# Fewer idle products around chunk 0, and modulation rows picked from 32 rows

## The chip, the cores and the metric

The kernel runs on one core of one Trainium2 chip. The metric is device time in microseconds (us): the time of one execution on the core. For the kernel before, three timed runs gave 661.33, 662.86 and 663.32 us; the median is 662.86 us.

A core has five engines that run side by side and wait for one another through semaphores: PE (TensorE, matrix products), DVE (VectorE), ACT (ScalarE), POOL (GpSimd) and SP (SyncE, which here issues nearly all DMAs). PE reads from the on-chip memory SBUF and writes to PSUM, where DVE and ACT fetch its results.

## The reference

One sequence of S = 2048 positions and D = 640 channels. A condition vector c gives six modulation rows of 640 values each; two blocks follow, each with its own layer norm, scale, shift and gate.

```python
mod = (_silu(c) @ w_mod).reshape(c.shape[0], 6, 1, -1)
sa, ca, ga, sb, cb, gb = (mod[:, 0], mod[:, 1], mod[:, 2], mod[:, 3], mod[:, 4], mod[:, 5])
h = _layernorm(x, axis=-1) * (1 + ca) + sa
x = x + ga * _A_ref(h, A_k, A_v, A_shift_k, A_ssm_k, A_ssm_D)
h = _layernorm(x, axis=-1) * (1 + cb) + sb
x = x + gb * _B_ref(h, B_w1, B_b1, B_w2, B_b2)
```

`_A_ref(q, k, v, ...)` runs a short convolution of four taps over k, multiplies by v, convolves each channel over the whole sequence with its own kernel of 2048 values (by an FFT), adds kv times a per-channel D, and multiplies by q. `_B_ref` is an MLP over the sequence axis: 2048 to 1728, GELU, and back.

## The kernel before, in words

All data are float32. An f32 product on PE leaves two pairs of records in the trace (weight load and MATMUL, twice); products in the form fp32r, used in the MLP, leave one pair.

**Block A** works in five chunks of 128 channels. The long convolution is a transform in two steps, written as products with constant matrices:

- k*v of a chunk is made by `kv_ops` (DVE, partly POOL; every elementwise product and sum of two tensors goes through the helper on L57). Its scratch on DVE is the PSUM tile `tap`: columns 0 to 512 hold a running sum, columns 512 to 768 the four taps, which `taps()` writes (ACT, L174).
- Step one, `step1(side, t)` (PE L223, ACT copies the result out on L229): four groups t for the k*v side (0) and four for the kernel side (1). The kernel side reads tile `p`, which `perm` (ACT, L168) fills.
- Step two, `f2(g)` for g = 0 to 7 (PE L242): 32 products each. ACT copies half of the result to `kt` (L246), DVE multiplies (`mul`, two products into `p`), and POOL or DVE adds into `y`.
- Back: `i2(r)` for r = 0, 1 (PE L271; ACT copies out on L280, DVE in one case on L278), then `i1(half)` for two halves (PE L291). `gate` (DVE, then POOL) multiplies by the normalized and modulated q, which `a1_ops` prepares (ACT L298, DVE), and adds to x.

The pieces of neighbouring chunks are interleaved by hand in the loop over c: during chunk c, DVE makes the k*v of a later chunk, taken piece by piece from the list `fill` by `dv(n)`; at the end of a turn step one of the next chunk's kernel runs. PSUM has four buffers of 1024 columns: `tap`, and three that `psum()` hands out in turn, so a product waits until the readers of the buffer's last contents are done.

**Modulation.** `mod_load` (SP, L344) loads w_mod in five parts; `mod_part` (PE L356) sums the products with silu(c) in `tap`, with each of three modulation rows held alike in 32 partitions, at partitions 0, 32 and 64; `mod_sum` (ACT L360) copies them to SBUF. `mod_row(i)` (PE L367) spreads row i over all 128 partitions by a product with a selection column from `pick`: two products, one for each half of 320 columns. Rows 0 to 2 are made at the end of chunk 0; rows 3 to 5 after chunk 4.

**Idle products.** `idle(n, ps)` (PE L350) issues n f32 products of 128 columns whose results nobody reads. In the turn of chunk 0 they stand ahead of `i2(0)`, and ahead of and behind the second `i1`, all writing to `tap`; in chunk 4 ahead of `mod_part`. A loop on L863 issues 34 fp32r products of 320 columns ahead of block B's first products.

**Block B** then runs the MLP as products of matrices split into high and low parts (PE L450, L990, L1307, L1384), from about 282 us to the end.

What sets the order: the program's own order on each engine, since the schedule is written by hand; SP issues its DMAs in that order too, each when its target is free.

Of the kernel before, what the change touches and what calls it, by code (L numbers as in the profile page):

```python
# [47 lines left out]
def mixer_kernel(ctx: ExitStack, tc: tile.TileContext, q, k, v, shift_k, ssm_k, ssm_D, w1, b1, w2, b2, c,  # L48
# [7 lines left out]
    act, dve, pool, pe, sync = nc.scalar, nc.vector, nc.gpsimd, nc.tensor, nc.sync  # L56
    TT = lambda eng, o, a, b, op: eng.tensor_tensor(o, a, b, op=op)  # L57
    uid = [0]
# [8 lines left out]
    def psum(slot=None):  # L67

        uid[0] += 1
        slot = ring[uid[0] % len(ring)] if slot is None else slot  # L70
        return psp.tile([128, 1024], F32, name=f"pst_{uid[0]}", tag=f"pst{slot}", bufs=1)
# [28 lines left out]
    F1, V2, ID, OWN = SM[:, 0:256], SM[:, 256:384], SM[:, 384:420], SM[:, 420:422]  # L100
# [6 lines left out]
    def small(n):  # L107
        so[0] += n
        assert so[0] <= 736
        return sm[:, so[0] - n:so[0]]  # L110
# [3 lines left out]
    bst = small(16 * 5 * 6).rearrange("p (j s k) -> p j s k", j=16, s=5)  # L114
    mv = small(32).rearrange("p (j k) -> p j k", j=16)
    rs1, nm1, rs2, nm2, tm = small(16), small(16), small(16), small(16), small(16)
    pick = small(64)
    su, sq, msb = small(16), small(16), small(1)
    epsc = small(1)
    B1C, B2C = cols[:, 0:14], cols[:, 14:30]  # L120
# [1 line left out]
    tap = psp.tile([128, 1024], F32, name="tap", tag="pst3", bufs=1)  # L122
# [92 lines left out]
    def step1(side, t, later=False, x=X, last=False):  # L215

        ps = psum()
        for a in range(8):
            i = 8 * t + a
            lhs = KSP[:, i] if side else x.rearrange("p (i m) -> p i m", i=32)[:, i]  # L220
            o = 256 * (a // 2) + a % 2
            for ri in range(2):
                pe.matmul(ps[64 * ri:64 * ri + 64, o:o + 255:2], lhs, F1[:, 128 * ri:128 * ri + 128], start=True,  # L223
                          stop=True)
        cut = (0, 32, 128) if t == 3 and last else (0, 128)

        def evac():
            for k0, k1 in zip(cut, cut[1:]):
                act.activation(Z[:, side, t, :, k0:k1], ps.rearrange("p (a k e) -> p a k e", a=4, e=2)[:, :, k0:k1], AF.Copy)  # L229
        return evac if later else evac()  # L230

    def f2(g):

        ps = psum()
        for kk in range(8):
            k1 = 8 * g + kk
            for ri in range(2):
                for h in range(2):
                    o = 128 * kk + 64 * ri
                    rhs = bass.AP(tensor=T_z.tensor, offset=T_z.offset + 64 * k1 + 32 * h,  # L240
                                  ap=[T_z.ap[0], [4096, 2], [1, 32]])
                    pe.matmul(ps[64 * h:64 * h + 64, o:o + 64], W2[k1 // 32][:, 2 * (k1 % 32) + ri], rhs, start=True, stop=True)  # L242
        pv = ps.rearrange("p (m s i) -> p m s i", s=2, i=32)
        xs_ = pv[:, :, 0]
        kt = KT[g % 2]
        act.activation(kt.rearrange("p (m i) -> p m i", i=32), pv[:, :, 1], AF.Copy)  # L246
        pa, pb = P[:, 1024 * (g % 2):1024 * (g % 2) + 512], P[:, 1024 * (g % 2) + 512:1024 * (g % 2) + 1024]
        m16 = lambda t: t.rearrange("p (m i) -> p m i", i=32)

        def mul():  # L250
            TT(dve, m16(pa), xs_, m16(kt), ALU.mult)
            sw = bass.AP(tensor=kt.tensor, offset=kt.offset + 32, ap=[kt.ap[0], [64, 8], [-32, 2], [1, 32]])
            TT(dve, pb.rearrange("p (k r i) -> p k r i", k=8, r=2), xs_.rearrange("p (k r) i -> p k r i", r=2), sw,
               ALU.mult)

        def add(eng=pool):
            for ri, t, op in ((0, pa, ALU.subtract), (1, pb, ALU.add)):
                t = t.rearrange("p (k r i) -> p r k i", k=8, r=2)
                TT(eng, Y[:, ri, :, 8 * g:8 * g + 8].rearrange("p i k -> p k i"), t[:, 0], t[:, 1], op)
        return mul, add  # L260
# [86 lines left out]
    def idle(n, ps):  # L347

        for _ in range(n):
            pe.matmul(ps[:, 0:128], F1[:, 0:128], F1[:, 128:256], start=True, stop=True)  # L350

    def mod_part(ps, kk, place):

# [9 lines left out]
    def mod_row(i, t, slot=None, later=False):  # L363

        ps, j = psum(slot).rearrange("p (h m) -> p h m", h=2), i % 3
        for h in range(2):
            pe.matmul(ps[:, h, 0:320], pick[0:96, j:j + 1].to_broadcast([96, 128]),  # L367
                      t[0:96, 320 * h:320 * h + 320], start=True, stop=True)
        ps = ps[:, :, 0:320]
        two = lambda t: t.rearrange("p (h m) -> p h m", h=2)  # L370
        if later:
            return lambda: act.activation(two(GB), ps, AF.Copy)
        if i == 0:
            act.activation(two(G0), ps, AF.Copy)
        elif i == 1:
            act.activation(two(G1), ps, AF.Copy, bias=1.0)
        elif i == 2:
            TT(dve, two(G0), ps, two(G0), ALU.mult)
            TT(dve, two(G1), ps, two(G1), ALU.mult)
        elif i == 3:  # L380
            act.activation(two(SB), ps, AF.Copy, accum_out=msb)
        elif i == 4:
            dve.tensor_scalar(two(CB), ps, 1.0, None, op0=ALU.add)
# [70 lines left out]
    piece = lambda t, n: [t[:, 640 * i:640 * i + 640] for i in range(n)]  # L454
    stg = T_g[0:36, 0:128]
    dve.memset(stg, 0.0)
    dve.memset(pick[0:96, 0:3], 0.0)
    for j in range(3):
        dve.memset(pick[32 * j:32 * j + 1, j:j + 1], 1.0)
    dve.memset(epsc, EPS)  # L460
    for h in range(2):
        dve.memset(KX[64 * h:64 * h + 1, 0:3, :], 0.0)
# [39 lines left out]
    ps = psum()  # L502
# [63 lines left out]
    for c in range(NC):  # L566
# [1 line left out]
        ac, po = a1_ops(c)  # L568
        pend_m = pend_a = None
        for g in range(8):  # L570
            m_, a_ = f2(g)
            if pend_m:
                pend_m()
            if pend_a:
                pend_a()
            pend_a, pend_m = (pend_m and pa_next), m_
            pa_next = a_
            if c:
                for f_ in ac[2 * g:2 * g + 2]:
                    f_()  # L580
            elif 0 < g < 5:
                w2_part(1, (g - 1) % 2, 32 * ((g - 1) // 2), 32)
                if g == 4:
                    load_q(range(4))
                    sync.dma_start(T_v1[:, 0:2048], c_v1, max_dma_last_dim=2048)
                    load_q(range(4, 8))
                    for kk in range(2):
                        mod_load(0, kk, homes[kk])
            if cn is None:

                t, o = (X, T_aux)[g // 4], 512 * (g % 4)
                act.activation(t[:, o:o + 1], epsc, AF.Copy)
                for b in range(2):
                    sync.dma_start(t[64 * b:64 * b + 64, o:o + 512],
                                   dram(w1, (16 * b + g) * F, [[32 * F, 64], [1, 512]]))
            if c == 1 and 1 < g < 6:
                late[g + 2]()
            dv(-(-len(fill) // max((6 if c else 8) - g, 1)))
            if c and cn is not None and g == 3:
                perm_add(cn)  # L600
            if cn == NC - 1 and g in turns:
                mod_third(turns[g])
# [13 lines left out]
        if c == 0:  # L616
# [3 lines left out]
            ps = psum()  # L620
# [1 line left out]
            act.activation(cols, ps[:, 0:36], AF.Copy)  # L622
            act.activation(sil, cols[:, 30:35], AF.Silu)
            step1(0, 1)
            idle(5, tap)
            i2(0)
            step1(0, 2)
            i2(1)
            k0 = step1(0, 3, True)
            for kk in range(4):  # L630
# [48 lines left out]
        if c:  # L679
            dv(7 if cn is not None else 8)  # L680
            if cn == NC - 1:
                mod_third(2)
            i2(0)
            if cn is None:
                split_rows(1, T_aux[:, 0:2048], (0, 1, 3))
                idle(4, psum((uid[0] + 1) % 3))
                uid[0] += 2
                mod_part(tap, 3, pl[3])
                i2(1, dve)
                t = mem("y", 4096, "wb2")  # L690
                blk[2] = j16(t[:, 0:2048]), j16(t[:, 2048:4096])
                break
            run(po)
            if cn == NC - 1:
                mod_third(3)
            step1(0, 2)
            if cn == NC - 1:
                mod_third(4)
            i2(1)
            step1(0, 3)  # L700
            dv(3)
# [3 lines left out]
        if cn == NC - 1:  # L705
            mod_third(5)
        for half in range(2):
            if c == 0 and half:
                idle(5, tap)
            ps = i1(half)  # L710
            if c == 0 and half:
                idle(4, tap)
            if c and half:
                dv(3)
            elif c:
                k0 = step1(1, 0, True)
            elif half:
                run(po[2:4])
            gate(c, ps, half)
# [35 lines left out]
    start = []  # L755
# [103 lines left out]
    ring[:] = [3, s1, s2, s0]  # L859
    uid[0] += 3 - uid[0] % 4  # L860
    acc.append(psum().rearrange("p (h m) -> p h m", h=2))
    for i in range(34):
        pe.matmul(acc[0][:, i % 2, 0:320], blk[0][0][:, 0].bitcast(F32R),  # L863
                  blk[1][0].rearrange("p j m -> p (j m)")[:, 0:320].bitcast(F32R), start=True, stop=True)
    x1_stats(range(2, 4))
# [587 lines left out]
```

## Time and profile before

| what | before |
|---|---|
| timed runs, median (lowest to highest) | 662.86 us (661.33 to 663.32) |
| the profiled execution's own time | 665.26 us |
| its span, first to last instruction | 663.3 us |
| mean granted clock of TensorE | 0.994 |
| busy share PE / DVE / ACT / POOL | 95% / 81% / 50% / 19% |
| idle products L350 (f32, 128 columns) | 36 records |
| `mod_row` products L367 | 24 records |
| products of L863 | 34 records |

How to read it: a row of a timeline gives start and length in us, engine, line, operation, what is written and read, the shape and type, and a count; in brackets stands the engine's idle time before it and who ended it ("issue" if the profile shows nobody). "PE" rows are the products and "PEld" the weight loads, which overlap them. A window row gives each engine's busy time with its instruction count (PE, PEld, DVE, ACT, POOL), then the granted clock of TensorE, the DMA share and GB/s. The chain of waits is followed back from the last instruction, at each step to what released it.

### The profile page before, as it was taken

The numbers are of one execution on the slowest core, as the hardware profiler recorded it, in microseconds if no ns is written. First come the engines' busy times: TensorE is split into PE (matmuls) and PEld (weight loads), VectorE is DVE, ScalarE is ACT, GpSimd is POOL, SyncE is SP. The second block draws the span as 40 slices with busy tenths as digits, with TensorE's granted clock in tenths as the row PEclk, the third lists the DMA queues.
The fourth block names the chain that finished last, engine by engine and source line by source line (L and its number), as shares of the span: only waits on it lengthen the run. The fifth ranks groups of instructions, "written<-read, shape, count | busy, mean of one in ns | idle before, by whom it ended". The sixth has DMA issues, their size and how long they took to land.

```text
span 663.3 us, 21125 instructions
## 1 busy us (share of the span) xinstructions
PE 627.7 (95%) x9131; PEld 590.6 (89%) x9131; DVE 536.3 (81%) x933; ACT 329.7 (50%) x547; POOL 127.0 (19%) x143
## 2 busy tenths in 40 slices
PE   6989779899999999898999999999999999999997
PEld 2878469899999998698997999999999999999997
DVE  7789668979979569799986976576799779888895
ACT  1664365646647655566777553345453133333331
POOL 5762027524226044000000000000000530000000
PEclk9999889999999999999999999999999999999999
DMA  9988997447432336171317342346832726346601
GB/s 188 223 226 244 330 183 159 97 79 165 88 80 82 102 95 185 41 159 32 64 33 223 116 118 80 81 105 173 266 106 57 203 88 194 109 130 172 190 31 40
DMA packets 173516, 88.46 MB, mean 133 GB/s; under 512 B 92430, under 2 KB 163632, under 8 KB 173424
## 3 DMA queue, kind: packets, MB, share of 16 engines
q1 hardware_dynamic: 166252, 85.53, 50.1%
q10 hardware_dynamic: 6916, 1.31, 1.2%
q8 instruction: 71, 1.16, 0.7%
q0 software_dynamic: 256, 0.28, 0.2%
q14 instruction: 21, 0.17, 0.1%
HBM read 73.01 MB, written 14.09 MB: 131 GB/s over the span
## 4 chain that ended last, share of the span: by engine, by line
PE 60%; DVE 21%; DMA 8%; ACT 4%; issue 3%; SPq 3%; ACTq 0%; DVEq 0%
PE pst L1307 16%; PE pst L990 10%; PE pst L1384 7%; PE pst L450 6%; PE pst L223 6%; PE pst L271 5%; PE pst L242 4%; PE pst L291 3%; DVE p L57 3%; SPq L535 2%; DVE tap L57 2%; DMA p<-in_w_mod_dram 2%; DMA xb<-in_A_q_dram 2%; ACT z L280 2%; DVE kt L57 2%
## 5 line engine op out<-in xcount | busy, mean ns | idle before, releaser
L242 PE MATMUL pst<-z,w 128*64 128x64 f32 x2560 | 78.9, 223 | 9.5 <-DVE p L57 4.4
L242 PEld LDWEIGHTS pst<-z,w 128*64 128x64 f32 x2560 | 76.7, 138 | 12.2 <-issue 8.3
L229 ACT ACTIVATE z<-pst 128x1024 f32<-128x1024 f32 (+2 forms) x45 | 43.3, 975 | 41.7 <-PE pst L223 41.6
L57 POOL TENSOR_TENSOR y<-p 128x256 f32<-128x256 f32 x72 | 51.3, 742 | 41.8 <-DVE p L57 41.5
L57 DVE TENSOR_TENSOR p<-pst,kt 128x512 f32<-128x512 f32 x80 | 50.7, 681 | 9.5 <-ACT kt L246 9.4
L1307 PE MATMUL pst<-r_z,m_w 128*128 128x320 f32 x222 | 41.6, 309 | 0.1
L271 PEld LDWEIGHTS pst<-v,y 32*128 32x128 f32 x1280 | 38.2, 187 | 3.8 <-issue 2.9
L271 PE MATMUL pst<-v,y 32*128 32x64 f32 x1280 | 40.3, 272 | 0.7 <-issue 0.5
L974 ACT ACTIVATE s_w<-s_w 128x768 fp32r<-128x768 f32 (+1 forms) x26 | 21.8, 838 | 36.8 <-DVE s_w L57 12.1
L246 ACT ACTIVATE kt<-pst 128x512 f32<-128x512 f32 x40 | 23.9, 597 | 31.0 <-PE pst L242 16.0
L1295 ACT ACTIVATE m_w<-m_v 128x896 fp32r<-128x896 f32 x24 | 22.7, 951 | 32.3 <-PE pst L1307 16.8
L57 DVE TENSOR_TENSOR s_w<-s_w,s_w 128x768 fp32r<-128x768 f32 (+1 forms) x26 | 24.6, 945 | 16.8 <-ACT s_w L974 12.1
L223 PE MATMUL pst<-v,p 128*64 128x128 f32 x640 | 37.4, 274 | 0.3 <-issue 0.2
L223 PEld LDWEIGHTS pst<-v,p 128*64 128x64 f32 x640 | 35.1, 137 | 2.0 <-issue 1.4
L57 DVE TENSOR_TENSOR tap<-tap,kt 128x512 f32<-128x512 f32 x51 | 35.5, 696 | 1.3
L1307 PEld LDWEIGHTS pst<-r_z,m_w 128*128 128x128 f32 x222 | 34.8, 188 | 0.4 <-DVE m_w L57 0.4
L280 ACT ACTIVATE z<-pst 128x512 f32<-128x512 f32 x38 | 21.1, 649 | 25.0 <-PE pst L271 25.0
L223 PE MATMUL pst<-v,x 128*64 128x128 f32 x512 | 30.8, 275 | 1.3 <-DVE x L57 0.9
L57 DVE TENSOR_TENSOR m_w<-m_v,m_w 128x896 fp32r<-128x896 f32 x24 | 27.9, 1167 | 3.3 <-ACT m_w L1295 2.9
L57 DVE TENSOR_TENSOR kt<-in,tap 128x512 f32<-128x512 f32 x42 | 28.8, 685 | 1.2
L223 PEld LDWEIGHTS pst<-v,x 128*64 128x64 f32 x512 | 27.8, 137 | 2.1 <-POOL y L57 1.0
L450 PE MATMUL pst<-r_z,wb 128*128 128x320 f32 x180 | 28.1, 311 | 1.5 <-DVE aux L57 1.3
(373 smaller groups left out, 1564.9 us busy)
## 6 DMA issues: line engine op xcount, KB each, us to landing
m_x<-xs SPq DMA_DIRECT2D x28, 160.0 KB
out_dram<-m_x SPq DMA_DIRECT2D x28, 160.0 KB
aux<-in_A_ssm_k_dram SPq DMA_DIRECT2D x8, 512.0 KB
m_v<-in_B_w_dram SPq DMA_DIRECT2D x9, 448.0 KB
x<-in_B_w_dram SPq DMA_DIRECT2D x7, 448.0 KB
s_w<-in_B_w_dram SPq DMA_DIRECT2D x16, 192.0 KB
in<-in_A_v_dram SPq DMA_DIRECT2D x22, 128.0 KB
x<-in_B_w_dram SPq DMA_DIRECT2D x22, 128.0 KB
```

What stands on the lines that cost most here:

```text
L57: TT = lambda eng, o, a, b, op: eng.tensor_tensor(o, a, b, op=op)
L223: pe.matmul(ps[64 * ri:64 * ri + 64, o:o + 255:2], lhs, F1[:, 128 * ri:128 * ri + 128], start=True, stop=True)
L229: act.activation(Z[:, side, t, :, k0:k1], ps.rearrange("p (a k e) -> p a k e", a=4, e=2)[:, :, k0:k1], AF.Copy)
L242: pe.matmul(ps[64 * h:64 * h + 64, o:o + 64], W2[k1 // 32][:, 2 * (k1 % 32) + ri], rhs, start=True, stop=True)
L246: act.activation(kt.rearrange("p (m i) -> p m i", i=32), pv[:, :, 1], AF.Copy)
L271: pe.matmul(pp[qd // 2][:, o:o + 64], Y[p, ri, i:i + 2].rearrange("p i k -> p (i k)"), V2[p, 64 * ri:64 * ri + 64], start=ri == 0, stop=ri ...
L280: act.activation(o, i, AF.Copy)
L450: pe.matmul(ps[0:m, h, 0:320], w_.bitcast(F32R), r_[:, 320 * h:320 * h + 320].bitcast(F32R), start=first and i == 0, stop=last and i == 2)
L990: pe.matmul(o, w_.bitcast(F32R), r_.bitcast(F32R), start=first and k == 0, stop=last and k == 2)
L1295: act.activation(W[n][0].bitcast(F32R), A[p, w_], AF.Copy)
L1307: pe.matmul(bank[n], w[:, i].bitcast(F32R), r.bitcast(F32R), start=i == 0 and k == 0, stop=i == 6 and k == 2)
L1384: pe.matmul(acc[s][:, h, 0:320], w[:, f_].bitcast(F32R), u[r + h].bitcast(F32R), start=f_ == 0 and k == 0, stop=f_ == NF - 1 and k == 2)
```

## The change

Five edits:

1. `idle` writes to columns 768 to 896 of the buffer that it is given, instead of 0 to 128.
2. In chunk 0, `f2(3)` begins with three idle products. Ahead of `i2(0)` five are gone; ahead of `i2(1)` two are new. The five ahead of the second `i1` and the four behind it are gone.
3. In chunk 4, two idle products stand ahead of `mod_part` instead of four.
4. The loop on L863 issues 31 products instead of 34.
5. `pick` becomes one column, with a 1 in partitions 0, 32 and 64; `mod_row` reads 32 partitions, beginning at 32 j for row j, instead of 96.

The diff:

```diff
--- before.py
+++ after.py
@@ -114,7 +114,7 @@
     bst = small(16 * 5 * 6).rearrange("p (j s k) -> p j s k", j=16, s=5)
     mv = small(32).rearrange("p (j k) -> p j k", j=16)
     rs1, nm1, rs2, nm2, tm = small(16), small(16), small(16), small(16), small(16)
-    pick = small(64)
+    pick = small(64)[:, 0:1]
     su, sq, msb = small(16), small(16), small(1)
     epsc = small(1)
     B1C, B2C = cols[:, 0:14], cols[:, 14:30]
@@ -229,9 +229,10 @@
                 act.activation(Z[:, side, t, :, k0:k1], ps.rearrange("p (a k e) -> p a k e", a=4, e=2)[:, :, k0:k1], AF.Copy)
         return evac if later else evac()
 
-    def f2(g):
+    def f2(g, n=0):
 
         ps = psum()
+        idle(n, ps)
         for kk in range(8):
             k1 = 8 * g + kk
             for ri in range(2):
@@ -347,7 +348,7 @@
     def idle(n, ps):
 
         for _ in range(n):
-            pe.matmul(ps[:, 0:128], F1[:, 0:128], F1[:, 128:256], start=True, stop=True)
+            pe.matmul(ps[:, 768:896], F1[:, 0:128], F1[:, 128:256], start=True, stop=True)
 
     def mod_part(ps, kk, place):
 
@@ -364,8 +365,8 @@
 
         ps, j = psum(slot).rearrange("p (h m) -> p h m", h=2), i % 3
         for h in range(2):
-            pe.matmul(ps[:, h, 0:320], pick[0:96, j:j + 1].to_broadcast([96, 128]),
-                      t[0:96, 320 * h:320 * h + 320], start=True, stop=True)
+            pe.matmul(ps[:, h, 0:320], pick[32 * j:32 * j + 32, 0:1].to_broadcast([32, 128]),
+                      t[32 * j:32 * j + 32, 320 * h:320 * h + 320], start=True, stop=True)
         ps = ps[:, :, 0:320]
         two = lambda t: t.rearrange("p (h m) -> p h m", h=2)
         if later:
@@ -454,9 +455,9 @@
     piece = lambda t, n: [t[:, 640 * i:640 * i + 640] for i in range(n)]
     stg = T_g[0:36, 0:128]
     dve.memset(stg, 0.0)
-    dve.memset(pick[0:96, 0:3], 0.0)
+    dve.memset(pick, 0.0)
     for j in range(3):
-        dve.memset(pick[32 * j:32 * j + 1, j:j + 1], 1.0)
+        dve.memset(pick[32 * j:32 * j + 1, 0:1], 1.0)
     dve.memset(epsc, EPS)
     for h in range(2):
         dve.memset(KX[64 * h:64 * h + 1, 0:3, :], 0.0)
@@ -568,7 +569,7 @@
         ac, po = a1_ops(c)
         pend_m = pend_a = None
         for g in range(8):
-            m_, a_ = f2(g)
+            m_, a_ = f2(g, 3 if c == 0 and g == 3 else 0)
             if pend_m:
                 pend_m()
             if pend_a:
@@ -622,9 +623,9 @@
             act.activation(cols, ps[:, 0:36], AF.Copy)
             act.activation(sil, cols[:, 30:35], AF.Silu)
             step1(0, 1)
-            idle(5, tap)
             i2(0)
             step1(0, 2)
+            idle(2, tap)
             i2(1)
             k0 = step1(0, 3, True)
             for kk in range(4):
@@ -683,7 +684,7 @@
             i2(0)
             if cn is None:
                 split_rows(1, T_aux[:, 0:2048], (0, 1, 3))
-                idle(4, psum((uid[0] + 1) % 3))
+                idle(2, psum((uid[0] + 1) % 3))
                 uid[0] += 2
                 mod_part(tap, 3, pl[3])
                 i2(1, dve)
@@ -705,11 +706,7 @@
         if cn == NC - 1:
             mod_third(5)
         for half in range(2):
-            if c == 0 and half:
-                idle(5, tap)
             ps = i1(half)
-            if c == 0 and half:
-                idle(4, tap)
             if c and half:
                 dv(3)
             elif c:
@@ -859,7 +856,7 @@
     ring[:] = [3, s1, s2, s0]
     uid[0] += 3 - uid[0] % 4
     acc.append(psum().rearrange("p (h m) -> p h m", h=2))
-    for i in range(34):
+    for i in range(31):
         pe.matmul(acc[0][:, i % 2, 0:320], blk[0][0][:, 0].bitcast(F32R),
                   blk[1][0].rearrange("p j m -> p (j m)")[:, 0:320].bitcast(F32R), start=True, stop=True)
     x1_stats(range(2, 4))
```

## The prediction

> **What bounds the kernel now.** I read the page first, then the chain of waits, then the timelines of the engines around each edited place, then their windows.
>
> ```profile
> span 663.3 us, 21125 instructions
> PE 627.7 (95%) x9131; PEld 590.6 (89%) x9131; DVE 536.3 (81%) x933; ACT 329.7 (50%) x547; POOL 127.0 (19%) x143
> q8 instruction: 71, 1.16, 0.7%
> ```
>
> PE, 95% busy, carries the kernel on average, so a removed product could be worth its full time. But each place has its own limit. The last row is PE's code: 2 x 9131 instructions in 71 packets make 257 instructions, some 128 pairs of weight load and product, to a packet.
>
> The chain of waits around chunk 0's end:
>
> ```profile
> 68.05 13.52 DMA p<-in_w_mod_dram
> ...
> 87.88 3.96 ACT aux L298 x10
> 91.84 0.52 ACT tap L174
> ...
> 94.74 2.62 PE pst L291 x121
> 97.35 1.09 PE tap L350 x8
> ```
>
> Up to 81.57 us the chain is a load of w_mod; PE is not on it. Then it runs through ACT's L298 and `taps` (L174) into PE's idle products (L350), `i1(1)` (L291) and four more idle products. PE's timeline there (an f32 product leaves two records):
>
> ```profile
> 35.02 5.82 PE L242 MATMUL pst<-z,w 128*64 128x64 f32 x192 [0.50 <-ACT z L229]
> 43.26 10.31 PE L242 MATMUL pst<-z,w 128*64 128x64 f32 x320 [2.43 <-issue]
> ...
> 58.42 1.38 PE L350 MATMUL tap<-v 128*128 128x128 f32 x10
> 59.74 4.09 PE L271 MATMUL pst<-v,y 32*128 32x64 f32 x128
> ...
> 69.04 1.57 PE L271 MATMUL pst<-v,y 32*128 32x64 f32 x49 [0.49 <-issue]
> ...
> 78.97 2.42 PE L356 MATMUL tap<-in,sm 128*32 128x320 f32 x12 [1.21 <-DMA in<-in_w_mod_dram]
> ...
> 84.06 3.50 PE L367 MATMUL pst<-kt,sm 96*128 96x320 f32 x12 [0.81 <-ACT kt L360]
> 87.48 2.10 PE L291 MATMUL pst<-z,v 64*64 64x64 f32 x128
> 92.40 2.34 PE L350 MATMUL tap<-v 128*128 128x128 f32 x10 [2.82 <-ACT tap L174]
> ...
> 98.37 7.21 PE L223 MATMUL pst<-v,p 128*64 128x128 f32 x128
> ```
>
> `i1(0)` ends at 89.58. The five idle products of the second half write tile `tap`, which `taps` is just writing, so they wait 2.82 us for ACT: padding meant to fill a gap makes one. They then take 2.34 us, where the same ten records took 1.38 at 58.42. The clock explains it:
>
> ```profile
> 40.00:45.00 5.00, 2.57 (x89) 2.53 (x85) 3.57 (x7) 2.36 (x3) 2.84 (x4) 1.00 0.75 165
> ...
> 85.00:90.00 5.00, 4.58 (x138) 3.45 (x136) 2.25 (x3) 4.19 (x10) 0.35 (x1) 1.00 1.05 194
> 90.00:95.00 5.00, 2.60 (x22) 2.38 (x26) 4.83 (x5) 4.46 (x8) 1.66 (x1) 0.76 1.18 192
> 95.00:100.00 5.00, 5.00 (x166) 4.81 (x160) 4.86 (x4) 0.00 (x0) 2.44 (x2) 0.90 0.81 166
> ...
> 115.00:120.00 5.00, 2.71 (x86) 2.48 (x83) 4.93 (x9) 1.59 (x5) 4.49 (x7) 1.00 0.03 7
> ...
> 275.00:280.00 5.00, 4.56 (x208) 3.74 (x206) 4.41 (x14) 3.41 (x7) 0.00 (x0) 1.00 0.01 3
> ```
>
> The granted clock (third number from the end; the DMA share follows) is 0.76, then 0.90: at half speed that is 2.4 + 1.0 = 3.4 us. It cost 0.96 us on the idle products and 0.52 on `i1(1)` (2.62 against 2.10). The gap of 2.43 at 43.26 left the clock at 1.00.
>
> What this lateness is worth is read on DVE:
>
> ```profile
> 87.65 1.56 DVE L57 TENSOR_TENSOR g<-pst,g 128x640 f32<-128x640 f32 x2 [7.90 <-ACT aux L298]
> ...
> 97.67 1.23 DVE L57 TENSOR_TENSOR aux<-pst,aux 128x1024 f32<-128x1024 f32 x1
> ...
> 106.07 0.70 DVE L57 TENSOR_TENSOR tap<-tap,kt 128x512 f32<-128x512 f32 x1
> 108.84 1.29 DVE L57 TENSOR_TENSOR p<-pst,kt 128x512 f32<-128x512 f32 x2 [2.07 <-ACT kt L246]
> ```
>
> From 87.65 DVE works without a break to 106.77, then waits 2.07 us for step two of chunk 1, which comes from PE through ACT. Afterwards it is full again (4.93 of 5 in the window 115 to 120). So PE may come earlier by anything; only 2.07 us of it are worth time.
>
> **The change, part by part.** *Last turn of chunk 0.* Without idle products `i1(1)` follows `i1(0)` at 89.58 with 128 pairs to do in 2.10 us. Its PSUM buffer last held a modulation row, which ACT reads ahead of the L298 group in the chain above. Next limit: code. The stalls marked "issue" at 43.26 and 69.04 stand 634 pairs apart, 4.9 packets, so both are packet starts. Counted on from 69.04, a packet starts 24 pairs before the end of `i1(0)`, at 89.2, and the next 105 pairs into `i1(1)`, reached at 91.3. How long after entering a packet is the next one there? At 43.26: entered 64 pairs into the row of 35.02, at 37.0, so 6.3 us, DMA share 0.75. At 280.42 (chunk 4, rows below): entered 74 pairs into the row of 276.31, at 277.5, so 2.9 us, DMA share 0.01. Hence code for the rest of `i1(1)` at 92.1 to 95.5; I take the middle, 93.8. Then 23 pairs (0.4 us), and step one of chunk 1's kernel (four groups of 7.21/4 = 1.80 us), whose input ACT has half done one copy after `taps`:
>
> ```profile
> 92.29 2.17 ACT L168 ACTIVATE p<-aux 128x1024 f32<-128x1024 f32 x2
> ```
>
> Two groups end at 97.8; the third needs the buffer that DVE frees at 97.67 + 1.23 = 98.90; the fourth ends at 102.5. Before, it ended at 105.58 and DVE's product began 3.26 us later. So that product can begin at 105.8, and DVE is ready at 106.77: **2.07 us gained**, PE 1.0 us ahead. If the clock drops again in the gap from 91.3 to 93.8, 1.7 us are lost, but the third group waited from 97.8 to 98.9, so 0.6 arrive and PE is still 0.4 ahead.
>
> The row against this is the clock's: a gap of 2.82 brought a drop. The Trainium skill, "TensorE: Matmul & The Clock Gate", section "Why this matters for your kernels", asks for no PE gap above about 3 us, which speaks for idle products. By it 2.5 us would be harmless, and so would 2.82 have been; the trace says otherwise, and the measurement decides. The sum is 2.07 by either; the first rival's chance is larger by the row.
>
> *Rows picked from 32 rows.* A modulation row costs four records of 3.50/12 = 0.29 us; row, column count and passes stay. Successive rows now use other row groups of the array. Products that rotate over row groups (59.74) take 0.032 us each for 64 columns, while full-array ones (58.42) take 0.138 for 128, so 0.069 for 64: neighbours in different groups overlap. Here the group changes only at two borders, so between nothing and 2 x 0.29 = 0.58 is saved. I take half, **0.29**. DVE starts 0.09 after the last of them, so it passes on.
>
> The Trainium skill, same page, "Part 3: Packing small matmuls — row/col tiling", says that a product of 32 rows alone takes as long as one of 128, and that only distinct row groups run at once. By that both borders vanish: 0.58 here, 0.30 below, and a time of 659.6 as an estimate.
>
> *Ahead of 81.57.* Three idle products before `f2(3)` add 6 x 0.138 = 0.83 us; five fewer before `i2(0)` take 1.38 away; two more before `i2(1)` add 0.55. Sum 0.00. The cover is the w_mod load: PE waits 1.21 us for its fourth part alone (78.97), and without that cover the 0.83 would show until `i2(0)`. Step two's idle products queue behind the code stall at 43.26, so they fill no gap. `tap` at columns 768 to 896 instead of 0 to 128 moves work off columns that DVE's k*v uses; nobody waits there. The smaller memset: nothing.
>
> *Chunk 4.*
>
> ```profile
> 264.23 1.16 PE L350 MATMUL pst<-v 128*128 128x128 f32 x8
> ...
> 267.38 0.70 PE L356 MATMUL tap<-z,sm 128*32 128x320 f32 x2 [0.79 <-issue]
> ...
> 273.96 2.42 PE L367 MATMUL pst<-t,sm 96*128 96x320 f32 x8
> 276.31 3.25 PE L291 MATMUL pst<-z,v 64*64 64x64 f32 x202
> 280.42 0.57 PE L291 MATMUL pst<-z,v 64*64 64x64 f32 x22 [0.86 <-issue]
> 281.86 5.39 PE L863 MATMUL pst<-wb,wb 128*128 128x320 f32 x34
> ...
> 295.18 4.40 PE L450 MATMUL pst<-r_z,wb 128*128 128x320 f32 x28 [1.33 <-DVE aux L57]
> ```
>
> PE is the chain here. Two idle products fewer save at most 0.55; nothing if the code stall 1.2 us later just grows. The packet start moves 22 pairs further on, so more work is done before it: I take **0.30**. The two rows at 273.96 have one border, nothing to 0.30: **0.15**; DVE's slack allows it, for it waits for the product that follows:
>
> ```profile
> 278.01 0.96 DVE L57 TENSOR_TENSOR aux<-pst,aux 128x768 f32<-128x768 f32 x1 [0.38 <-PE pst L291]
> ```
>
> 31 instead of 34 products at 281.86 free 3 x 0.159 = 0.48 us, but PE later waits 1.33 for DVE (295.18); that wait grows: 0.
>
> **Sum:** 2.07 + 0.29 + 0.30 + 0.15 = 2.81 us. The profiled execution took 665.26 (span 663.3 and 2.0 around it), so 662.45; the median of the runs is 2.4 lower, 662.86, and gives **660.0 us**.
>
> **Rivals.** *The code comes late and the clock falls.* Code at 95.5 means a gap of 4.2 us; then 0.4 + 7.2 us of work with 1.7 lost ends at 104.8, DVE's product begins at 108.1, and the wait shrinks by 0.8 only: total 1.5, 661.3. For it: DMA share 1.05 to 1.18 at that time. Chance 0.15.
>
> *The clock had not dropped in most runs of before.* Without the drop PE was 1.48 us earlier and DVE waited 0.59: total 1.3, 661.5. For it: the lowest run, 661.33, lies 1.53 under the median. Against: the median and the highest, 663.32, lie together. Chance 0.18.
>
> *Slower: code stalls move onto the chain.* Net nine products, 36 instructions, fewer shift every later packet start by 18 pairs. In chunk 1 code was already late:
>
> ```profile
> 149.45 0.81 PE L223 MATMUL pst<-v,p 128*64 128x128 f32 x11 [0.18 <-issue]
> ```
>
> One new stall between 0.49 and 2.43, say 1.46, in each of chunks 1 to 3, where PE is the chain, costs 4.4: 664.5. It decides once the three together exceed 2.81. Against: the packets there are no shorter than before. Chance 0.07.
>
> *The edit doesn't free `i1(1)`*, since it waits for something that the idle products' wait hid. Even started at 92.40 it would end at 94.5 without code stall, so little is lost; with one, it joins the first rival: 661.3. Chance 0.03.
>
> **How the numbers follow.** The forecast keeps 0.57. About 0.3%, 2.0 us, can be told from no change; faster is below 660.9. The forecast's own range is 2.07 to 3.5 us of gain, 659.4 to 660.8, so faster 0.57; the middle rivals are the same, 0.36; slower 0.07. The range runs from 658.9 (all upper bounds, 0.5 for the runs' spread) to 662.4 (rivals with every small term at zero, and the same spread).
>
> **What would show it.** Right: no L350 between `i1(0)` and step one of chunk 1; DVE's wait near 106.8 gone; a PE "issue" gap inside `i1(1)`; 10 or 11 records' time for the twelve of L367. Wrong: DVE still waits for kt there; clock 0.76 in the windows after 95; new "issue" gaps between 125 and 255; an unshifted chunk 4.

## The result, and the profile after

The changed kernel takes 659.36 us (median of 22 runs, 656.71 to 665.12); the kernel before, run beside it, 664.53 us (22 runs, 661.33 to 671.17). The ratio is 0.9922, with a 95% interval of 0.9900 to 0.9944: 5.2 us faster (3.7 to 6.6). The forecast, 660.0 against 662.86, was a ratio of 0.9957, 2.9 us. The direction was right, the gain too small. That 659.36 lies so near the forecast's 660.0 is luck: the forecast started from a median of three runs that was 1.7 us below this one of 22.

The page of the kernel after:

```profile
span 663.3 us, 21074 instructions
...
PE 627.2 (95%) x9106; PEld 592.7 (89%) x9106; DVE 536.4 (81%) x933; ACT 329.5 (50%) x547; POOL 127.9 (19%) x143
...
q8 instruction: 71, 1.16, 0.7%
```

PE has 25 products' records fewer (22 of L351, 3 of L860), in still 71 packets of code. The span equals that before, 663.3 us: this profiled execution, 665.12 us, is the slowest of the 22. PE's timeline and the windows (granted clock third from the end of a row) show why:

```profile
65.13 1.12 PE L272 MATMUL pst<-v,y 32*128 32x64 f32 x12 [2.38 <-issue]
...
70.94 7.11 PE L272 MATMUL pst<-v,y 32*128 32x64 f32 x128
```

```profile
65.00:70.00 5.00, 4.87 (x45) 4.42 (x45) 4.83 (x16) 2.25 (x5) 0.00 (x0) 0.50 1.00 329
70.00:75.00 5.00, 5.00 (x80) 4.78 (x84) 2.27 (x8) 0.96 (x1) 0.00 (x0) 0.50 1.04 397
75.00:80.00 5.00, 5.00 (x80) 4.88 (x78) 0.00 (x0) 1.92 (x4) 0.00 (x0) 0.50 0.75 284
80.00:85.00 5.00, 5.00 (x52) 2.73 (x51) 2.87 (x7) 3.40 (x7) 1.36 (x2) 0.79 0.02 5
```

A code stall inside `i2(0)` was followed by half the clock until past 80 us, and `mod_row` began at 88.20 instead of 84.06. So the two spans can't be compared; stretches that begin at `mod_row` can. The turn after that point, on PE:

```profile
88.20 2.27 PE L368 MATMUL pst<-kt,sm 32*128 32x320 f32 x12 [0.82 <-ACT kt L361]
90.40 3.60 PE L292 MATMUL pst<-z,v 64*64 64x64 f32 x228
95.55 0.68 PE L292 MATMUL pst<-z,v 64*64 64x64 f32 x28 [1.56 <-issue]
97.16 3.71 PE L223 MATMUL pst<-v,p 128*64 128x128 f32 x64 [0.92 <-ACT p L168]
102.22 3.71 PE L223 MATMUL pst<-v,p 128*64 128x128 f32 x64 [1.35 <-DVE aux L57]
```

`i1(1)` follows `i1(0)` without a gap, code stalls it after 100 of its 128 pairs (228 records less the 128 of `i1(0)`), and step one now waits for ACT and for DVE, 0.92 and 1.35 us: PE is ahead. The modulation rows take 2.27 us instead of 3.50. On DVE:

```profile
90.56 1.56 DVE L57 TENSOR_TENSOR g<-pst,g 128x640 f32<-128x640 f32 x2 [3.43 <-PE pst L368]
...
109.24 0.70 DVE L57 TENSOR_TENSOR tap<-tap,kt 128x512 f32<-128x512 f32 x1
109.85 1.28 DVE L57 TENSOR_TENSOR p<-pst,kt 128x512 f32<-128x512 f32 x2
```

The wait of 2.07 us ahead of step two's first product `p<-pst,kt` is gone. In chunk 4:

```profile
264.78 0.71 PE L351 MATMUL pst<-v 128*128 128x128 f32 x4
...
268.28 3.34 PE L272 MATMUL pst<-v,y 32*128 32x64 f32 x108 [0.31 <-issue]
...
273.92 1.35 PE L368 MATMUL pst<-t,sm 32*128 32x320 f32 x8
...
281.41 1.34 PE L368 MATMUL pst<-t,sm 32*128 32x320 f32 x4 [1.91 <-DVE sm L788]
282.68 6.34 PE L860 MATMUL pst<-wb,wb 128*128 128x320 f32 x31
```

The two rows cost 1.35 instead of 2.42, the code stall 0.31 instead of 0.79, and the last row, which waited for nobody before, waits 1.91 for DVE.

Four stretches, each from the trace: A from the start of `mod_row` in chunk 0 to DVE's first `p<-pst,kt` of chunk 1 (before: 108.84 - 84.06 = 24.78); B from there to the end of chunk 4's step two; C from there to the 101st product record of L451 in block B (L450 before); D from there to the end. "Early code" are kernels with the kernel before's count of PE instructions ahead of chunk 1, so that code packets start at its places there; in "late code" they start 18 pairs further on.

| kernel | code | A | B | C | D | ratio to before, 95% interval |
|---|---|---|---|---|---|---|
| before | early | 24.78 | 148.23 | 49.18 | 357.10 | |
| e1 before, again | early | 23.23 | 148.68 | 49.63 | 357.11 | 0.9995 (0.9971 to 1.0019) |
| e2 rows alone | early | 25.39 | 149.97 | 49.14 | 357.11 | 1.0006 (0.9978 to 1.0033) |
| e3 turn alone | late | 22.71 | 148.60 | 48.70 | 357.14 | 0.9941 (0.9911 to 0.9972) |
| e4 rows and turn | late | 22.76 | 148.24 | 48.43 | 356.75 | 0.9948 (0.9916 to 0.9980) |
| after | late | 21.65 | 147.78 | 48.50 | 357.13 | 0.9922 (0.9900 to 0.9944) |
| e5 after, again | late | 21.64 | 148.03 | 48.33 | 357.14 | 0.9922 (0.9888 to 0.9956) |
| e6 after, front of before | late | 21.65 | 147.77 | 48.26 | 357.13 | 0.9897 (0.9858 to 0.9936) |
| e7 after, rows of before | late | 22.62 | 148.16 | 48.22 | 357.12 | 0.9941 (0.9910 to 0.9972) |
| e8 padding without the wait | 8 pairs on | 25.07 | 147.99 | 48.25 | 357.13 | 0.9977 (0.9942 to 1.0012) |
| e9 after, 9 products at the start | early | 22.75 | 148.25 | 48.87 | 357.13 | 0.9958 (0.9937 to 0.9980) |
| e10 before, 55 at the start | late | 26.00 | 147.72 | 48.45 | 357.12 | 1.0222 (1.0194 to 1.0249) |
| e11 chunk 4 alone | early | 23.24 | 148.59 | 51.45 | 357.15 | 0.9997 (0.9968 to 1.0026) |
| e12 after, third row elsewhere | late | 21.09 | 148.58 | 48.28 | 357.29 | 0.9936 (0.9913 to 0.9959) |

From `mod_row` to the end the two profiles of before took 579.29 and 578.65 us, the two of after 575.06 and 575.14: 3.9 us less. By means, 2.4 of it lie in A, 0.6 in B and 1.0 in C. The rest of the measured 5.2 lies within its interval, or ahead of `mod_row`, where executions of one kernel differ by 4 us (after: 88.20 and 84.06).

### The profile page after: what moved, and what is told of

The parts are those of the page before. It is cut to its first block, busy times and chain, and to the rows that moved or that the text cites. A ratio compares the mean times of both kernels' runs of the same rounds, so it can differ in the third digit from the quotient of the medians.

```text
span 663.3 us, 21074 instructions
## 1 busy us (share of the span) xinstructions
PE 627.2 (95%) x9106; PEld 592.7 (89%) x9106; DVE 536.4 (81%) x933; ACT 329.5 (50%) x547; POOL 127.9 (19%) x143
## 4 chain that ended last, share of the span: by engine, by line
PE 62%; DVE 23%; DMA 5%; issue 4%; ACT 4%; SPq 2%; DVEq 0%; ACTq 0%
PE pst L1304 16%; PE pst L987 10%; PE pst L1381 7%; PE pst L223 7%; PE pst L451 6%; PE pst L272 6%; PE pst L243 5%; DVE p L57 3%; DVE tap L57 2%; PE pst L292 2%; DVE kt L57 2%; DMA xa<-in_const_w_dram 1%; DVE sm L566 1%; PE pst L1046 1%; DVE aux L57 1%
## 5 line engine op out<-in xcount | busy, mean ns | idle before, releaser
L272 PEld LDWEIGHTS pst<-v,y 32*128 32x128 f32 x1280 | 41.8, 202 | 6.0 <-issue 5.4
L272 PE MATMUL pst<-v,y 32*128 32x64 f32 x1280 | 44.0, 288 | 2.8 <-issue 2.7
L223 PE MATMUL pst<-v,x 128*64 128x128 f32 x512 | 34.2, 293 | 1.4 <-DVE x L57 1.0
L223 PEld LDWEIGHTS pst<-v,x 128*64 128x64 f32 x512 | 30.9, 148 | 2.3 <-POOL y L57 1.1
L451 PE MATMUL pst<-r_z,wb 128*128 128x320 f32 x180 | 28.0, 310 | 0.1
```

The costliest lines, as they stand in the source:

```text
L272: pe.matmul(pp[qd // 2][:, o:o + 64], Y[p, ri, i:i + 2].rearrange("p i k -> p (i k)"), V2[p, 64 * ri:64 * ri + 64], start=ri == 0, stop=ri ...
L451: pe.matmul(ps[0:m, h, 0:320], w_.bitcast(F32R), r_[:, 320 * h:320 * h + 320].bitcast(F32R), start=first and i == 0, stop=last and i == 2)
```

## The experiments

Five theories are weighed: the *turn* (idle products that waited for `taps` held `i1(1)` back, and DVE paid for it), the *rows* (they cost less than one border each), the *code* (removed instructions shift the packet starts, so stalls in later chunks come or go), the *front* (idle products moved ahead of the w_mod load are worth nothing), and the *clock* (the changed kernel's clock falls less often). In the expectations of e2 to e4, theory A is the turn and rows that run side by side as wholes, theory B the clock.

**e1, the kernel before again**, no edit.

> The kernel before, unchanged, to see how far its own executions differ. Both theories: no difference, a ratio of 1 with an interval that holds it. If the granted clock falls at other places in this profile than at 79 and 92.6 us, the first profile's wait of 2.07 us on DVE is not the usual one: without a drop behind i1(0) it would be 0.6.

Idle products of the turn and DVE's first product of step two:

```profile
92.42 1.38 PE L350 MATMUL tap<-v 128*128 128x128 f32 x10 [2.83 <-ACT tap L174]
```

```profile
107.30 1.29 DVE L57 TENSOR_TENSOR p<-pst,kt 128x512 f32<-128x512 f32 x2 [0.50 <-ACT kt L246]
```

After the same wait, 2.83 us, the clock did not fall this time: 1.38 instead of 2.34 us, and DVE waited 0.50 instead of 2.07. What the turn costs the kernel before thus differs from execution to execution: 2.07 here and 0.50 there, 2.30 in e2, 2.32 in e10, 0.51 in e11.

**e2, the rows alone; e3, the turn alone; e4, both.**

```diff
-            pe.matmul(ps[:, h, 0:320], pick[0:96, j:j + 1].to_broadcast([96, 128]),
-                      t[0:96, 320 * h:320 * h + 320], start=True, stop=True)
+            pe.matmul(ps[:, h, 0:320], pick[32 * j:32 * j + 32, 0:1].to_broadcast([32, 128]),
+                      t[32 * j:32 * j + 32, 320 * h:320 * h + 320], start=True, stop=True)
```

```diff
-            if c == 0 and half:
-                idle(5, tap)
             ps = i1(half)
-            if c == 0 and half:
-                idle(4, tap)
```

> Only the modulation rows read 32 rows; all idle products stay. Theory A, rows of different row groups run side by side as wholes: twelve records of the chunk-0 rows take 2.3 us instead of 3.5, and eight in chunk 4 take 1.35 instead of 2.4. DVE begins 1.0 us earlier, but the idle products still wait for the taps, which ACT reaches only 0.5 earlier, so 0.5 there and 0.4 in chunk 4 (DVE's 0.38 us of slack): 0.9 us faster, ratio 0.9986. Theory B, the gain beyond the forecast came from fewer clock drops: rows are worth the forecast 0.3 to 0.4 us, ratio 0.9994.

> Only the nine idle products of chunk 0's last turn are gone. Theory A: DVE's wait of 2.07 us before step two of chunk 1 is gone and nothing else moves: 2.1 us faster, ratio 0.9969; a code stall of about 2 us about 105 pairs into the second i1. Theory B: the clock no longer drops in that stretch, and this alone gives most of the measured 5.2 us: 4 us or more, ratio 0.994 or below.

> Both of these together, the rest as before. Theory A: more than the two alone, since the earlier DVE start now reaches step two: 2.07 + 1.05 at the turn and 0.4 in chunk 4, 3.5 us, ratio 0.9947. Theory B: what the idle products alone give, plus 0.4.

PE in e2:

```profile
83.36 2.27 PE L367 MATMUL pst<-kt,sm 32*128 32x320 f32 x12 [0.81 <-ACT kt L360]
...
91.21 2.50 PE L350 MATMUL tap<-v 128*128 128x128 f32 x10 [3.56 <-ACT tap L174]
93.64 3.62 PE L291 MATMUL pst<-z,v 64*64 64x64 f32 x128
```

The rows are 1.23 us shorter, and the idle products' wait for `taps` grows from 2.82 to 3.56. So only 0.49 us gets past that wait: the idle products begin 7.85 us after the rows' start, instead of 8.34. Then the clock fell, for longer than in before (`i1(1)` takes 3.62 us, `i1(0)` 2.10), and A is no shorter. The total, 1.0006, shows no gain, but its interval is too wide to exclude half a microsecond. PE and DVE in e3:

```profile
92.30 0.68 PE L291 MATMUL pst<-z,v 64*64 64x64 f32 x28 [2.97 <-issue]
92.91 8.85 PE L223 MATMUL pst<-v,p 128*64 128x128 f32 x128
```

```profile
105.01 1.29 DVE L57 TENSOR_TENSOR p<-pst,kt 128x512 f32<-128x512 f32 x2
```

This execution met the forecast's bad case: a code stall of 2.97 us, then half the clock, step one at 8.85 instead of 7.21. DVE still waited for nothing. This kernel gives 0.9941, most of the gain, though not by the turn alone: nine idle products fewer make its code late too. In e4 the clock was down during the rows (12 records in 3.42), so its A shows no more than e3's.

Theory B is not borne out. The mean granted clock was 0.992 in the 84 executions of before that ran beside e1 to e12, and 0.992 in the 34 of after and e5. Among those with a clock of 0.996 or more, 14 of before took 661.84 to 666.05 us (median 662.91) and 9 of after and e5 656.71 to 660.75 (658.59). So the gain is there without a difference in the clock.

**e5, the kernel after again**, no edit.

> The changed kernel, unchanged, as the measure for the three beside it and for a second profile. Ratio 0.992 to the kernel before. If its first profile (clock at half from 65 to 82 us) was an unlucky execution, this one has no such stretch and a span near 657.5.

A is 21.64 (after: 21.65) and `mod_row` begins at 84.06: the long half clock ahead of 82 us belonged to one execution, not to the version. (In e5 the clock was down for less of that stretch: 1.00 from 65 to 70, 0.60 from 70 to 75, 0.72 from 75 to 80.)

**e6, after with the front of before.**

```diff
-            m_, a_ = f2(g, 3 if c == 0 and g == 3 else 0)
+            m_, a_ = f2(g)
...
+            idle(5, tap)
             i2(0)
             step1(0, 2)
-            idle(2, tap)
             i2(1)
```

> The changed kernel with the idle products ahead of chunk 0's modulation as before: none in step two, five ahead of the first i2, none ahead of the second. Forecast: this part is worth nothing, since the w_mod load covers it: the same time as the changed kernel, ratio 0.992. Rival: in most executions PE, late from a code stall, is the chain there, and this part carries what the forecast missed, 1 to 2 us: ratio 0.994 to 0.995.

0.9897, from A on the same times as after. What lies ahead of A differs by 4 us between executions of one kernel, so there only the totals can be compared. They show no gain by the three moves ahead of the w_mod load; the intervals would even allow a loss of some us, or a gain of one. The other columns for idle products (edit 1) were not run by themselves.

**e7, after with rows picked from 96**: e2's edit undone.

> The changed kernel with modulation rows picked from 96 rows as before. Whole rows side by side: 1.06 us lost at the turn and 0.4 in chunk 4, 1.5 us slower than the changed kernel, ratio 0.9944. Forecast: 0.44 slower, 0.9929.

A is 22.62 instead of 21.65: the rows are worth 0.97 us once nothing stands between them and DVE. The two rows in chunk 4 are read on DVE, first in e7, then in after:

```profile
275.23 0.96 DVE L57 TENSOR_TENSOR aux<-pst,aux 128x768 f32<-128x768 f32 x1 [0.37 <-PE pst L292]
```

```profile
277.51 0.96 DVE L57 TENSOR_TENSOR aux<-pst,aux 128x768 f32<-128x768 f32 x1
```

With rows of 96 DVE waits for the product behind them, as before did (0.38 us); with rows of 32 it doesn't. From its copy into `z` (L278 or L279) to its next wait for ACT, DVE takes 13.16 to 13.21 us with rows of 96 (e3, e7, e10) and 12.98 to 13.02 with rows of 32 (e4, after, e5, e6, e12), all with late code. So these two rows are worth 0.2 us. B and C as a whole don't show it: C of e7 is even shorter than after's, because the code stall of 0.31 us is missing in it. The ratio's interval does not separate e7 from after.

**e8, the padding kept, its wait taken away**: the five products go into `i1`'s own buffer, which is free, the four behind it are gone.

```diff
-    def i1(half, slot=None, js=range(8)):
+    def i1(half, slot=None, js=range(8), n=0):
         ps = psum(slot)
+        idle(n, ps)
...
-            if c == 0 and half:
-                idle(5, tap)
-            ps = i1(half)
-            if c == 0 and half:
-                idle(4, tap)
+            ps = i1(half, n=5 if c == 0 and half else 0)
```

> The kernel before, with the five idle products ahead of the second i1 written into that i1's own buffer instead of the taps' one, and the four behind it gone. If the wait for the taps was what cost: as without any of the nine, DVE's wait of 2.07 us is gone, 2 to 4 us faster, ratio 0.994 to 0.997, since PE has 1 us to spare and code is late there anyway. If the products' own 1.4 us on PE were the cost: less than 1 us faster, 0.9985 or more.

```profile
87.77 5.95 PE L368 MATMUL pst<-kt,sm 96*128 96x320 f32 x12 [0.81 <-ACT kt L361]
93.65 2.10 PE L292 MATMUL pst<-z,v 64*64 64x64 f32 x128
95.67 1.38 PE L351 MATMUL pst<-v 128*128 128x128 f32 x10
```

```profile
112.84 1.28 DVE L57 TENSOR_TENSOR p<-pst,kt 128x512 f32<-128x512 f32 x2
```

The ten records run for 1.38 us without a wait, and DVE does not wait either. The rows came at half the clock (5.95 instead of 3.50 us); A less these 2.45 is 22.62, e7's value. So it was the wait for `taps` that cost, not the 1.38 us of work. The total, 0.9977 (0.9942 to 1.0012), can't be told from either kernel.

**e9 and e10, the code's position alone.** Products that nobody reads, at the very start: 9 (18 pairs) in front of after put the packets back to before's places; 55 (110 pairs, that is 128 less 18) in front of before put them to after's.

```diff
+    for _ in range(9):
+        pe.matmul(ps[:, 512:520], T_in[0:1, 0:128], T_in[0:1, 128:136], start=True, stop=True)
```

> The changed kernel with nine tiny products (8 columns, 36 instructions) at the very start, while PE waits for its first load: every later code packet starts at the place in the program where it started before the change. If the shift of the packets is what shortened chunks 1 to 4: from DVE's first product in step two of chunk 1 to the end 554.5 to 555.5 us as in the kernel before (554.5 and 555.4) instead of 553.2 to 553.5, with code stalls of 0.2 to 0.6 us near 148, 166 and 266 us again; about 1.3 us slower than the changed kernel, ratio 0.994. If the edits themselves shortened them: 553.4, and no difference.

> The kernel before with 55 tiny products (220 instructions, which is 256 less 36) at the start, so that the later packets start where they do in the changed kernel. Packets: 553.4 us from DVE's first product in step two of chunk 1 to the end, 1 to 1.5 less than before, ratio 0.998. Edits: 554.5 to 555.4, ratio 1.

PE's stalls in chunks 1 and 4, first of e9, then of e11, which has the early code without any product added:

```profile
147.56 3.22 PE L223 MATMUL pst<-v,p 128*64 128x128 f32 x54 [0.99 <-issue]
...
277.92 0.56 PE L292 MATMUL pst<-z,v 64*64 64x64 f32 x18 [1.63 <-issue]
```

```profile
148.11 3.22 PE L223 MATMUL pst<-v,p 128*64 128x128 f32 x54 [0.90 <-issue]
...
281.34 0.56 PE L291 MATMUL pst<-z,v 64*64 64x64 f32 x18 [1.36 <-issue]
```

The padding brought back stalls at the very same places, with 54 and 18 records of the group left. B and C together take 197.12 us, 0.8 more than after (196.28). In B the profiles agree on the whole: PE's stalls marked "issue" add up to 0.35 to 1.78 us in the five kernels with early code, and to 0 to 0.64 in the eight with late code. A is longer by 1.1, because the rows ran at half the clock (12 records in 3.42 us), so of the total, 0.9958, only a part is the code's. PE of e10:

```profile
1.66 23.63 PE L504 MATMUL pst<-in 1*128 1x8 f32 x110 [1.66 <-DVE in L462]
25.21 13.84 PE L506 MATMUL pst<-in 128*128 128x512 f32 x28
...
295.85 0.33 PE L291 MATMUL pst<-z,v 64*64 64x64 f32 x4 [1.01 <-issue]
```

Its total failed as an experiment: the 55 products were meant to run while the input was loading, but a record of 8 columns took 23.63/110 = 0.21 us, more than the 0.138 of an idle product's 128 columns, so the first real product began at 25.2 instead of 5.6. The stretches behind it answer the question: between 100 and 295 us not one "issue" stall is left, and B and C take 196.17, as in after (196.28), against 197.41 in before and 198.31 in e1, though none of after's edits is in this kernel.

**e11, chunk 4 alone.**

```diff
-                idle(4, psum((uid[0] + 1) % 3))
+                idle(2, psum((uid[0] + 1) % 3))
...
-    for i in range(34):
+    for i in range(31):
```

> The kernel before with only the chunk-4 edits: two idle products ahead of the modulation part instead of four, 31 instead of 34 ahead of block B. Forecast: 0.30 us for the first, nothing for the second, ratio 0.9995. From the end of chunk 4's step two to the modulation part 7.7 us (end of the idle products or of the load, whichever is later) instead of 8.25; the wait for DVE near 295 us grows by 0.5.

0.9997 (0.9968 to 1.0026): nothing to be told from no change. The trace gives no more, since the clock fell in this very place, first shown by PE and then by a window:

```profile
270.32 2.36 PE L356 MATMUL tap<-p,sm 128*32 128x320 f32 x12
```

```profile
268.00:272.00 4.00, 4.00 (x63) 2.78 (x57) 1.29 (x2) 1.14 (x2) 0.00 (x0) 0.54 0.00 0
```

But e8 and e10, which have neither of these edits nor the rows, reach C = 48.25 and 48.45, and after 48.50 and 48.33. So most of C's gain needs none of chunk 4's edits: it comes by code stalls. What the two idle products fewer give is too small to be seen beside the 0.45 us by which C differs between before and e1. PE in e1, with four of them, and in after, with two:

```profile
263.13 1.16 PE L350 MATMUL pst<-v 128*128 128x128 f32 x8
264.70 1.27 PE L356 MATMUL tap<-z,sm 128*32 128x320 f32 x10 [0.40 <-DMA z<-in_w_mod_dram]
```

```profile
265.87 1.28 PE L357 MATMUL tap<-z,sm 128*32 128x320 f32 x12 [0.38 <-DMA z<-in_w_mod_dram]
```

In both, PE then waits for a load of w_mod, so the idle products stand in front of a wait. Counted from the end of step two, `mod_part` goes on at 8.24 to 8.76 us with four of them (seven profiles) and at 8.08 to 8.39 with two (seven as well).

**e12, towards a better kernel**: e6, with the third row in buffer `tap`, so that it need not wait for ACT to free one, and half of ACT's other work of the turn put earlier.

```diff
-            run(ac[0:4])
+            run(ac[0:8])
...
-                mod_row(i, T_kt[:, 0:640])
-            run(ac[4:16])
+                mod_row(i, T_kt[:, 0:640], ps=tap if i == 2 else None)
+            uid[0] += 1
+            run(ac[8:16])
```

> The changed kernel with the idle products ahead of the modulation as before, the third modulation row made in the taps' buffer, so that it needn't wait for ACT's copy of the last step-one group, and eight instead of four of chunk 0's normalized q pieces made before the rows. Whole rows side by side: the twelve records of chunk 0's rows take 1.6 us instead of 2.27, DVE's wait of 0.32 for ACT goes, 0.5 to 1.0 us less from the rows' start to DVE's first product of step two (21.65 now), ratio 0.990 to 0.992. If three row groups don't run together as two do: 2.27 and 0.3 us less.

```profile
83.99 0.54 PE L368 MATMUL pst<-kt,sm 32*128 32x320 f32 x2 [0.82 <-ACT kt L361]
84.03 0.53 PE L368 MATMUL tap<-kt,sm 32*128 32x320 f32 x1
84.37 0.44 PE L368 MATMUL pst<-kt,sm 32*128 32x320 f32 x2
84.40 0.43 PE L368 MATMUL tap<-kt,sm 32*128 32x320 f32 x1
...
86.12 3.60 PE L292 MATMUL pst<-z,v 64*64 64x64 f32 x228 [0.76 <-ACT g L375]
```

All three rows run side by side and take 1.37 us. A falls by 0.55 to 21.09, but B is 0.8 longer than e6's, with two code stalls (0.45 and 0.20 us) where e6 has none; the time, 0.9936 (0.9913 to 0.9959), is no better than after's.

## Why the forecast was right in direction and too small

*The turn: right.* The padding's wait held `i1(1)` back; with the wait gone (e8) or the padding gone (e3), DVE's wait is gone. Its size was read from one execution: 2.07 us where the clock fell, 0.50 where it didn't. That is the second rival's condition; it held in two of five profiles of kernels with the old turn (e1, e11), not in most. Its 0.59 rests on 2.62 us for `i1(1)`, which in the chain are 121 of its 128 records; with the timeline's 2.69 for all of them it is 0.52, and e1 and e11 have 0.50 and 0.51.

*Code inside `i1(1)`: right.* The stall was forecast 105 pairs in and came 100 in; with rows of 96 it ended 10.0 (e3) and 9.4 us (e7) after the start of `mod_row`, forecast 93.8 - 84.06 = 9.7. In e3 the clock fell behind it, at a cost of 1.64 (forecast 1.7), and PE was still early enough. So the first rival's fall of the clock occurred, and did not decide.

*The rows: the term that was mis-sized.* "Here the group changes only at two borders, so between nothing and 2 x 0.29 = 0.58 is saved." Measured: 1.23 us on PE and 0.97 in A; the twelve records take the time of 8, where the forecast's sign was that of 10 or 11. The step took it that products start one after another, so that only neighbours at a border overlap. In fact whole rows run side by side: 2.27 us is the time of two rows in sequence, the third waiting for its buffer, and 1.37 that of little more than one. The Trainium skill, "TensorE: Matmul & The Clock Gate", "Part 3: Packing small matmuls — row/col tiling", says that products in different row groups run concurrently, with which this agrees; the forecast applied it to the borders alone.

*Chunk 4: one term right, one not.* The rows' 0.15 is borne out: 0.2 us on DVE (e7). The rest of the 1.07 us that they save on PE goes into the wait for DVE (1.91 us at 281.41). The idle products' 0.30 is not seen: the forecast weighed them against the code stall behind them and left out the load of w_mod, for which PE waits next. C fell by 1.0, but mostly by code.

*Code stalls in chunks 1 to 4: the sign.* "Net nine products, 36 instructions, fewer shift every later packet start by 18 pairs." That is what happened (e9, e10), but the shift took stalls away. Of the 1.5 us by which B and C became shorter, the code's place explains 0.8 by e9 and all by e10. The slower rival priced only the loss, and the sum had nothing for it; the same mechanism should have had both signs.

*The front:* 0.00 was forecast, and e6 shows no gain; its interval is too wide to say more.

With 2.4 in A, 0.6 in B and 1.0 in C, the trace holds 3.9 us (rounded) where the forecast's sum had 2.81. Which share of A's 2.4 an average execution owes to the clock's fall in before stays open: it takes the traces of more executions.

## What to carry to other kernels

An idle product must not wait for anything: write it to a buffer that nobody uses, or it makes the gap that it should fill. Products on 32 rows in different row groups and different PSUM buffers overlapped here as a whole, so free all their buffers first. A change in the number of PE instructions moves code stalls everywhere behind it: judge an edit by stretches of the trace, and have a kernel run that moves the code alone.

## What the runs showed of the hardware

- Products of different row groups don't start in program order. In e12 the third row's first record starts at 84.03, ahead of the first two rows' second ones at 84.37. The Trainium skill, "TensorE: Matmul & The Clock Gate", "Part 3: Packing small matmuls — row/col tiling", states that products start and end strictly in order; this trace disagrees as to the start, if the order is that of the kernel's text (the profile doesn't show another).
- A busy PE did not bring the clock back: after the stall that ended at 65.13 us, PE was busy for 4.87, 5.00 and 5.00 of 5 us in the windows from 65 to 80, at a clock of 0.50.
- Whether a gap lowers the clock is not fixed by its length: after 2.82 us it fell in before, after 2.83 it did not in e1. And in before the clock was also down, 0.90 from 75 to 80 us and 0.76 from 80 to 85, where PE's longest gap is the 1.21 us at 78.97.
- These tiny products weren't cheap: 0.21 us for a record with 8 columns (e10), at a granted clock of 1.00.
